# Storing every second split weight tile as one scaled float32 tile, splitting it again in the next block, and starting the later attention pairs one or two steps sooner

## The chip, the core and the metric

The kernel runs on one core of a Trainium2 chip. The core has five engines with a queue of instructions each: TensorE (PE, matmuls, with its weight loads shown apart as PEld), VectorE (DVE), ScalarE (ACT), GpSimd (POOL) and SyncE (SP). SP and POOL are used here to issue DMAs, which 16 DMA engines carry out. Work reaches an engine only when the semaphores that it waits for have been raised; an engine runs its own queue strictly in order, so an instruction that waits holds all that stand behind it. The metric is the time of one execution on the device, in microseconds, as the median of several runs.

## The reference

Attention with a learned bias of relative position, then two feed-forward layers, all in float32, for 4 batches, 8 heads, 576 positions and a head width of 64:

```python
scores = scale * np.matmul(q, k.transpose(0, 1, 3, 2))
x = (psi_rel / psi_i)[..., None]
h = np.maximum(x @ w1 + b1, 0.0)
scores = scores + (h @ w2).transpose(2, 0, 1)[None]
attn = np.exp(scores - max) ; attn = attn / (sum + 1e-09)
x = np.matmul(attn, v)                          # to [2304, 512]
gate = 1.0 / (1.0 + np.exp(-(x @ w_gate)))      # 512 -> 1536
x = (gate * (x @ w_val)) @ w_out                # 1536 -> 512
h = x @ w_in                                    # 512 -> 2048
out = (h * np.clip(h + 3.0, 0.0, 6.0) / 6.0) @ w_out2
```

## The kernel before

**Blocks.** The 576 query positions are cut into five chunks (128, 128, 128, 128, 64). For each chunk the attention of all heads and batches is computed, and the feed-forward layers then run over its tokens (512 for the first four, 256 for the last). The attention of the first chunk comes alone at the start (the lead, up to 82.8 us in the trace). After it, block k (`block`, line 953) runs the feed-forward layers of chunk k and, strewn between, the attention of chunk k + 1. Block 0 lasts from 82.80 to 329.37 us, block 1 to 563.83, block 2 to 788.97, block 3 to 993.42, block 4 to the end.

**Steps.** The feed-forward work of a block is 68 steps (`moe_steps`, line 41), each with one weight tile of 128 x 512: steps 0 to 23 are the gate and value products (G, V), 24 to 35 the first output product (Y), 36 to 45 and 54 to 59 the hidden products of the second layer (H 0 to 9 and 10 to 15), 46 to 53 and 60 to 67 its output products (O). Precision is kept by splitting every operand into a rounded part and a rest, so a product is three matmuls (line 656): rounded weight by rounded and rest of the activation, and rest of the weight by rounded activation. A step is four groups of three, twelve matmuls of 512 columns. After an H step ACT evicts the sum from PSUM (line 699), DVE forms the activation (line 700), ACT writes its rounded half gh (line 671) and DVE the rest gl (line 673). Step 61 multiplies the halves of steps 56 to 59.

**Weights.** In block 0 the weights arrive packed (wd, line 575, 512 KB a tile, a pool of 4 buffers, issued six steps ahead). `w_part` (line 592) unpacks and splits a tile in four parts: ACT scales the low bits into tpc or tpd; DVE joins them with the high bits into a plain float32 tile, in place in wd (line 607); ACT writes the rounded half of 256 times that tile into wp (lines 598 and 615); DVE writes the rest (line 618). The pair of halves in wp (a pool of 6 buffers, 512 KB) is used by the step and is also stored to memory, to wsp, by `w_store` on SP (line 634). In all later blocks `w_load` reads both halves back from wsp into wp on SP (line 581), five steps ahead; the load waits for PE's last use of the buffer. In block 0 a round of the loop issues a load for tile i + 6, the store of tile i + 2 and the split of tile i + 3.

**Attention pairs.** The attention of chunk 1, in block 0, is `chunk_att` (line 853): eight pairs of units, pair i starting at step `at[i]`. A pair's keys are split 2.1 steps before its start (`pair_split`, lines 341 and 342), its scores computed at the start, the bias added and the minimum taken by DVE (line 541), four exponentials by ACT (line 385), the division shared between ACT and DVE (lines 396 and 398), the transposes on PE (line 427) with ACT's copies out (line 431), and the product with the values (line 472) just before the next pair. The bias rows of chunk 1 are stored by POOL (line 226) and read back by SP for the first pair (line 284). In blocks 1 to 3 the transposes are done by DVE and 16 small DMAs per pair (pT, line 451), half of them or all on POOL, into one buffer that is free only after the previous pair's product.

**Order.** In block 0 the orders of PE and SP are as the program writes them; in the later blocks that of PE alone. The order of the other engines (ACT, DVE and POOL everywhere after the lead, SP in later blocks) is set when the kernel is built, by a planner that plays the program through with times of its own and lets each engine take what is ready first. Each engine then runs that order on the chip, whatever the real times are.

**Memory.** Pools are laid out one behind another. Those of the first block alone (`conv`, line 810) are closed after it, and their room is given to pools of the later blocks.

Of the kernel before, what the change touches and what calls it, by code (L numbers as in the profile page):

```python
# [9 lines left out]
F32 = mybir.dt.float32  # L10
F32R = mybir.dt.float32r
U32 = mybir.dt.uint32
# [4 lines left out]
ALU = mybir.AluOpType  # L17
# [44 lines left out]
def fused_kernel(ctx: ExitStack, tc: tile.TileContext, qd, kd, vd, tz, td, cst, iden, wpack, out):  # L62
# [28 lines left out]
        for c, (_, n) in enumerate(QC)  # L91
    ]
    wsp = dr_p.tile([NSTEP, 128, 2, 512], F32, name="wsp")

    tz_t = const.tile([128, 2 * S - 4], F32, name="tz_t")
    cst_t = const.tile([128, 3 + 32 + S // 4], F32, name="cst_t")
# [473 lines left out]
    def w_load(n):  # L570
        if n >= NC * NSTEP:
            return
        if n < NSTEP:
            wd = A["wf"].tile([128, 512, 2], U32, name="wd")
            nc.sync.dma_start(
                out=wd.rearrange("p a b -> p (a b)").bitcast(U16)[:, 0:2047], in_=wpack[n].bitcast(U16)[:, 1:2048]
            )
            wf_q[n] = wd
        else:
            wp = w_p.tile([128, 2, 4, 128], F32R, name="wp")  # L580
            nc.sync.dma_start(out=wp.rearrange("p s c m -> p s (c m)").bitcast(F32), in_=wsp[n % NSTEP])
            wq[n] = wp

    cm_q, tp_q = {}, {}
# [1 line left out]
    def w_tops(names):  # L586

        for x, name in enumerate(names):
            tp_q[x] = A["tp"].tile([128, 512], U32, name=name)
            nc.gpsimd.memset(tp_q[x], 0)  # L590

    def w_part(n, part):

        def scaled(out, x, by):
            if n < 2:
                nc.vector.tensor_scalar(out=out, in0=x, scalar1=by, scalar2=None, op0=ALU.mult)
            else:
                nc.scalar.activation(out=out, in_=x, func=AF.Copy, scale=by)  # L598

        wd = wf_q.get(n)  # L600
        if part == 0:
            top, low = (x.rearrange("p (a b) -> p a b", b=b) for x, b in (
                (wd.rearrange("p a b -> p (a b)").bitcast(BF16), 4), (tp_q[n % 2].bitcast(F16), 2)))
            scaled(low[:, :, 1], top[:, :, 2], 0.5)
        elif part == 1:
            cm_q[n] = wd[:, :, 0]
            nc.vector.scalar_tensor_tensor(
                out=cm_q[n], in0=wd[:, :, 0], scalar=13, in1=tp_q[n % 2],
                op0=ALU.logical_shift_right, op1=ALU.bitwise_or,
            )  # L610
            del wf_q[n]
        elif part == 2:
            wq[n] = w_p.tile([128, 2, 4, 128], F32R, name="wp")
            wv = wq[n].rearrange("p s c m -> p s (c m)")
            scaled(wv[:, 0], cm_q[n].bitcast(F32), 256.0)
        else:
            wv = wq[n].rearrange("p s c m -> p s (c m)")
            nc.vector.scalar_tensor_tensor(  # L618
                out=wv[:, 1], in0=cm_q.pop(n).bitcast(F32), scalar=256.0, in1=wv[:, 0].bitcast(F32),
                op0=ALU.mult, op1=ALU.subtract,  # L620
            )
            if n < 2:
                nc.sync.dma_start(out=wsp[n], in_=wv.bitcast(F32))
# [6 lines left out]
            w_part(n, part)  # L630

    def w_store(n):
        if 2 <= n < NSTEP:
            nc.sync.dma_start(out=wsp[n], in_=wq[n].rearrange("p s c m -> p s (c m)").bitcast(F32))


    ys, gs, accs, th_q, ps_q = {}, {}, {}, {}, {}
# [166 lines left out]
    def late(name, bufs):  # L804
        return pool(name, bufs, reuse_waits="tile")

    A["bo"] = late("bo", 1)
    P = dict(gu=late("gu", 12), tmp=late("tmp", 3), acc=late("acc", 4))
    A.update(k=late("k", 4), v=late("v", 4), s=late("s", 2))
    conv = ExitStack()  # L810
    for name, bufs in (("pt", 2), ("wf", 4), ("tp", 1), ("qs", 1)):
        A[name] = conv.enter_context(tc.tile_pool(name=name + "c", bufs=bufs, reuse_waits="tile"))
    ctx.enter_context(tc.issue_after(gate.ins))
    ctx.enter_context(tc.issue_after(gate_act.ins))
# [111 lines left out]
    def block_events(k):  # L926
        ev = []
        last = NSTEP - 1
        if k == 0:
            ev.append((1.0, lambda: nc.sync.dma_start(out=td_t[:, t0:], in_=td[:, t0:])))  # L930
            ev += chunk_bias(1, 1.0, 1.2, NG1 + 2)
            ev += chunk_att(1, (13, 20, 27, 33, 40, 46, 52, 58, 64))
        elif k == 1:
            d = (last - 21.0) / 9
            ev += chunk_bias4(2.0, 1.5)
# [17 lines left out]
    def block(k):  # L953
        ev = block_events(k)
        for i in range(NSTEP):
            while ev and ev[0][0] <= i:
                ev.pop(0)[1]()
            if k == 0 and i == NSTEP - 6:
                held.extend((issued[1], issued[2]))
            n = k * NSTEP + i  # L960
            if k == 0:
                if n + WA + 1 < NSTEP:
                    w_load(n + WA + 1)
                for x in range(WB - 1 if i == 0 else WB, WB + 1):
                    w_store(n + x - 1)
                    w_split(n + x)
                if i == 0:
                    for last in issued[1], issued[2]:
                        ctx.enter_context(tc.issue_after(last.ins))
            if n + WA >= NSTEP:  # L970
                w_load(n + WA)
            moe_step(k, i, P, mm_ps)
        for e in ev:
            e[1]()
# [1 line left out]
    with tc.manual_schedule(engines={ET.PE, ET.SP}):  # L976
        block(0)
    conv.close()
    A.update(ks=late("ks", 2), qs=late("qs", 2), t=late("t", 1), pt=late("pt", 1))
    with tc.manual_schedule(engines={ET.PE}), tc.issue_after(held[0].ins), tc.issue_after(held[1].ins):  # L980
        for k in range(1, NC):
            block(k)
# [64 lines left out]
```

## Time and profile before

| | |
|---|---|
| median of three runs | 1098.02 us (1096.3 to 1098.59) |
| profiled execution | 1096.07 us |
| its span | 1094.3 us |
| PE busy | 1082.1 us, 99% of the span |
| DVE, ACT, POOL busy | 645.8, 539.5, 131.7 us |
| DMA | 321.94 MB, 294 GB/s over the span |

The span runs from the first instruction of the program to its last; the execution's own time has 1.8 us around it. A matmul's end in the trace is modelled, and matmuls overlap in a pipeline, so the distance between the starts of two matmuls tells their pace, and the idle time of PE leaves a little of each late start out.

### The profile page before, as it was taken

The numbers are of one execution on the slowest core, as the hardware profiler recorded it, in microseconds if no ns is written. First come the engines' busy times: TensorE is split into PE (matmuls) and PEld (weight loads), VectorE is DVE, ScalarE is ACT, GpSimd is POOL, SyncE is SP. The second block draws the span as 40 slices with busy tenths as digits, with TensorE's granted clock in tenths as the row PEclk, the third lists the DMA queues.
The fourth block names the chain that finished last, engine by engine and source line by source line (L and its number), as shares of the span: only waits on it lengthen the run. The fifth ranks groups of instructions, "written<-read, shape, count | busy, mean of one in ns | idle before, by whom it ended". The sixth has DMA issues, their size and how long they took to land.

```text
span 1094.3 us, 19682 instructions
## 1 busy us (share of the span) xinstructions
PE 1082.1 (99%) x7042; PEld 880.4 (80%) x7042; DVE 645.8 (59%) x1530; ACT 539.5 (49%) x1066; POOL 131.7 (12%) x252
## 2 busy tenths in 40 slices
PE   9999999999999999999999999999999999999998
PEld 5777778888877787878788888788888888888897
DVE  7887777788863357886735654656252417154433
ACT  7888687798962435464523342534032214123332
POOL 2000000000010011121211111111430202031000
PEclk9999999999999999999999999999999999999999
DMA  7958999999996788999897878798995969588997
GB/s 245 354 192 314 397 357 367 381 314 386 390 333 233 234 275 283 303 305 315 286 316 254 288 253 274 244 281 244 282 295 206 304 211 286 199 254 302 369 375 269
DMA packets 118480, 321.94 MB, mean 294 GB/s; under 512 B 20720, under 2 KB 29424, under 8 KB 118384
## 3 DMA queue, kind: packets, MB, share of 16 engines
q1 hardware_dynamic: 107968, 297.09, 79.0%
q0 software_dynamic: 9152, 23.21, 7.6%
q8 instruction: 56, 0.92, 0.4%
q10 hardware_dynamic: 1264, 0.39, 0.2%
q14 instruction: 40, 0.33, 0.1%
HBM read 245.08 MB, written 51.37 MB: 271 GB/s over the span
## 4 chain that ended last, share of the span: by engine, by line
PE 83%; DMA 6%; ACT 5%; DVE 3%; issue 2%; SPq 0%; POOL 0%; DVEq 0%; ACTq 0%; POOLq 0%
PE ps L656 60%; PE ps L472 7%; PE ps L650 6%; PE ps L519 3%; DMA wsp<-wp 2%; PE ps L355 2%; PE ps L411 2%; PE ps L171 1%; DMA wd<-wpack 1%; ACT z L156 1%; ACT s L385 1%; PE ps L427 1%; DMA vt<-vd 1%; DMA biasD<-bo 1%; PE ps L525 1%
## 5 line engine op out<-in xcount | busy, mean ns | idle before, releaser
L656 PE MATMUL ps<-xyh,wp 128*128 128x512 f32 (+1 forms) x1472 | 428.9, 378 | 2.1 <-ACT wp L598 1.2
L656 PEld LDWEIGHTS ps<-xyh,wp 128*128 128x128 f32 x1472 | 263.4, 188 | 60.2 <-DVE m L541 2.7
L656 PE MATMUL ps<-gh,wp 128*128 128x512 f32 (+1 forms) x980 | 295.8, 384 | 1.1 <-ACT gh L671 1.1
L656 PE MATMUL ps<-xyl,wp 128*128 128x512 f32 x640 | 249.8, 390 | 0.4 <-DVE xyl L675 0.3
L656 PEld LDWEIGHTS ps<-gh,wp 128*128 128x128 f32 x980 | 178.8, 188 | 40.2 <-issue 2.7
L656 PE MATMUL ps<-gl,wp 128*128 128x512 f32 x448 | 175.0, 391 | 0.8 <-DVE gl L673 0.6
L451 POOL DMA_DIRECT2D pT<-t x192 | 94.4, 500 | 493.0 <-DVE t L441 153.2
L671 ACT ACTIVATE gh<-tmp 128x512 fp32r<-128x512 f32 (+1 forms) x140 | 82.1, 587 | 127.0 <-DVE tmp L694 85.0
L656 PEld LDWEIGHTS ps<-xyl,wp 128*128 128x128 f32 x640 | 120.3, 188 | 25.2 <-DVE xyl L675 1.3
L385 ACT ACTIVATE s<-s,m 128x576 f32<-128x576 f32 x144 | 110.2, 767 | 25.4 <-DVE m L541 24.0
L673 DVE TENSOR_TENSOR gl<-tmp,gh 128x512 fp32r<-128x512 f32 x112 | 76.7, 687 | 38.9 <-ACT gh L671 37.8
L656 PEld LDWEIGHTS ps<-gl,wp 128*128 128x128 f32 x448 | 84.2, 188 | 18.4 <-DVE gl L673 1.9
L472 PEld LDWEIGHTS ps<-pT,vt 128*64 128x64 f32 x1600 | 78.9, 137 | 12.9 <-issue 11.5
L472 PE MATMUL ps<-pT,vt 128*64 128x128 f32 (+1 forms) x1600 | 89.1, 265 | 0.1
L700 DVE SCALAR_TENSOR_TENSOR tmp<-tmp,ps 128x512 f32<-128x512 f32 (+1 forms) x80 | 50.1, 629 | 54.8 <-ACT tmp L699 53.2
L694 DVE SCALAR_TENSOR_TENSOR tmp<-tmp,ps 128x512 f32<-128x512 f32 x48 | 32.7, 682 | 74.7 <-PE ps L656 73.7
L699 ACT ACTIVATE tmp<-ps 128x512 f32<-128x512 f32 (+1 forms) x80 | 43.9, 549 | 43.9 <-PE ps L656 43.5
L398 DVE TENSOR_SCALAR s<-s,r 128x576 f32<-128x576 f32 x128 | 61.4, 516 | 1.9
L497 ACT ACTIVATE xyh<-ps 128x256 fp32r<-128x256 f32 (+1 forms) x44 | 15.2, 344 | 94.4 <-PE ps L472 94.4
L724 POOL DMA_DIRECT2D outT<-acc x40 | 27.7, 737 | 267.6 <-DVE acc L715 247.7
L618 DVE SCALAR_TENSOR_TENSOR wp<-wd,wp 128x512 fp32r<-128x512 f32 x68 | 46.7, 688 | 21.4 <-ACT wp L598 20.8
L541 DVE CUSTOM_DVE_ANT_0 s<-ps,bm,m 128x320 f32<-128x320 f32 x112 | 56.1, 545 | 0.0
(112 smaller groups left out, 1169.6 us busy)
## 6 DMA issues: line engine op xcount, KB each, us to landing
wp<-wsp SPq DMA_DIRECT2D x272, 512.0 KB, 5.3
wsp<-wp SPq DMA_DIRECT2D x68, 512.0 KB, 7.4
wd<-wpack SPq DMA_DIRECT2D x68, 511.8 KB, 7.0
vt<-vd SPq DMA_DIRECT2D x80, 320.0 KB, 5.5
kt<-kd SPq DMA_DIRECT2D x80, 288.0 KB, 5.8
pT<-t POOLq DMA_DIRECT2D x192, 72.0 KB, 4.9
pT<-t SPq DMA_DIRECT2D x128, 72.0 KB, 4.4
bm<-biasD SPq DMA_DIRECT2D x15, 576.0 KB, 6.2
```

Of the source, the lines that this page charges most:

```text
L385: nc.scalar.activation(out=s[:, h], in_=s[:, h], func=AF.Exp, scale=-1.0, bias=d["m"][:, h:h + 1], accum_out=r[:, h:h + 1],)
L398: nc.vector.tensor_scalar(out=s[:, h], in0=s[:, h], scalar1=r[:, h:h + 1], scalar2=None, op0=ALU.mult)
L451: (nc.sync if p[0][0] < 4 and i > 1 else nc.gpsimd).dma_start(out=pt[32 * q:32 * q + 32, i].rearrange("j u t i -> j (u t i)"), in_=t[32 * ...
L472: nc.tensor.matmul(out=po[64 * h:64 * h + 64, n * a:n * a + n], lhsT=vt[:, v], rhs=pt[:, m * a:m * a + m, k, :], start=(t == 0), stop=(t = ...
L541: nc.vector.tensor_tensor_reduce(out=d["s"][:, h, j0:j1], in0=x, in1=bm_q[c, hp][:, h, j0:j1], scale=-(D ** -0.5), scalar=top, op0=ALU.add ...
L618: nc.vector.scalar_tensor_tensor(out=wv[:, 1], in0=cm_q.pop(n).bitcast(F32), scalar=256.0, in1=wv[:, 0].bitcast(F32), op0=ALU.mult, op1=AL ...
L650: nc.tensor.matmul(out=o, lhsT=w[:, c, :], rhs=x, start=(first and c == 0 and w is wh), stop=(last and c == 3 and w is wh),)
L656: nc.tensor.matmul(out=ps[:, 0:nt], lhsT=w[:, c, :], rhs=x[:, 0:nt], start=(first and c == 0 and i == 0), stop=(last and c == 3 and i == 2),)
L671: nc.scalar.activation(out=hi, in_=src, func=AF.Copy, scale=scale)
L673: nc.vector.tensor_tensor(out=lo, in0=src, in1=hi.bitcast(F32), op=ALU.subtract)
L699: nc.scalar.activation(out=t, in_=ps, func=AF.Relu, bias=3.0)
L700: nc.vector.scalar_tensor_tensor(out=t, in0=t, scalar=6.0, in1=ps, op0=ALU.min, op1=ALU.mult)
```

## The change

For the 20 even tiles from 2 to 40 (`in_whole`), block 0 forms the plain float32 tile in a buffer of its own (cm, two buffers) and not in place in wd, and `w_store` stores that tile, 256 KB, to a new place in memory, wsf, where before both halves went to wsp. The split in block 0 stays. In block 1 the load of such a tile reads 256 KB from wsf into one half of wp. `w_again` splits it there, two steps ahead of its use: one ACT pass and one DVE pass of 128 x 512. `w_keep` then stores both halves to wsp, one step ahead of the use, on POOL's queue; blocks 2 to 4 read wsp as before.

In block 0 the starting steps of the attention pairs move: pairs 0 and 1 stay at 13 and 20, pairs 2 to 7 go from 27, 33, 40, 46, 52, 58 to 26, 32, 38, 44, 50, 56, and the end of the last from 64 to 63. The pool of keys has two buffers in block 0 instead of four, and is made anew, with four, for the later blocks.

```diff
@@ w_load
         else:
             wp = w_p.tile([128, 2, 4, 128], F32R, name="wp")
-            nc.sync.dma_start(out=wp.rearrange("p s c m -> p s (c m)").bitcast(F32), in_=wsp[n % NSTEP])
+            wv = wp.rearrange("p s c m -> p s (c m)").bitcast(F32)
+            if in_whole(n - NSTEP):
+                nc.sync.dma_start(out=wv[:, 1], in_=wsf[n - NSTEP])
+            else:
+                nc.sync.dma_start(out=wv, in_=wsp[n % NSTEP])
             wq[n] = wp
+    def in_whole(n):
+        return 2 <= n < 42 and n % 2 == 0
@@ w_part
         elif part == 1:
-            cm_q[n] = wd[:, :, 0]
+            cm_q[n] = A["cm"].tile([128, 512], U32, name="cm") if in_whole(n) else wd[:, :, 0]
@@ w_store
-        if 2 <= n < NSTEP:
+        if in_whole(n):
+            nc.sync.dma_start(out=wsf[n], in_=cm_q.pop(n).bitcast(F32))
+        elif 2 <= n < NSTEP:
             nc.sync.dma_start(out=wsp[n], in_=wq[n].rearrange("p s c m -> p s (c m)").bitcast(F32))
+    def w_again(n):
+        if in_whole(n - NSTEP):
+            wv = wq[n].rearrange("p s c m -> p s (c m)")
+            f = wv[:, 1].bitcast(F32)
+            nc.scalar.activation(out=wv[:, 0], in_=f, func=AF.Copy, scale=256.0)
+            nc.vector.scalar_tensor_tensor(
+                out=wv[:, 1], in0=f, scalar=256.0, in1=wv[:, 0].bitcast(F32), op0=ALU.mult, op1=ALU.subtract
+            )
+    def w_keep(n):
+        if in_whole(n - NSTEP):
+            nc.gpsimd.dma_start(out=wsp[n - NSTEP], in_=wq[n].rearrange("p s c m -> p s (c m)").bitcast(F32))
@@ pools
-    A.update(k=late("k", 4), v=late("v", 4), s=late("s", 2))
+    A.update(v=late("v", 4), s=late("s", 2))
-    for name, bufs in (("pt", 2), ("wf", 4), ("tp", 1), ("qs", 1)):
+    for name, bufs in (("pt", 2), ("wf", 4), ("tp", 1), ("qs", 1), ("k", 2), ("cm", 2)):
...
-    A.update(ks=late("ks", 2), qs=late("qs", 2), t=late("t", 1), pt=late("pt", 1))
+    A.update(k=late("k", 4), ks=late("ks", 2), qs=late("qs", 2), t=late("t", 1), pt=late("pt", 1))
@@ block_events
-            ev += chunk_att(1, (13, 20, 27, 33, 40, 46, 52, 58, 64))
+            ev += chunk_att(1, (13, 20, 26, 32, 38, 44, 50, 56, 63))
@@ block
             if n + WA >= NSTEP:
                 w_load(n + WA)
+                w_keep(n + 1)
+                w_again(n + 2)
             moe_step(k, i, P, mm_ps)
```

## Rows read from the trace of the kernel before

**Rows 1.** Page, part 1: busy time, share of the span, instructions.

```profile
PE 1082.1 (99%) x7042; PEld 880.4 (80%) x7042; DVE 645.8 (59%) x1530; ACT 539.5 (49%) x1066; POOL 131.7 (12%) x252
```

**Rows 2.** Busy time by stretch: length, PE, PEld, DVE, ACT, POOL; clock, DMA, GB/s.

```profile
82.80:329.37 246.57, 243.04 (x1516) 198.48 (x1515) 191.07 (x423) 198.47 (x359) 6.30 (x10) 1.00 0.98 360
...
329.37:455.00 125.63, 125.63 (x728) 99.63 (x727) 67.58 (x161) 51.64 (x98) 13.25 (x26) 1.00 0.79 260
...
455.00:563.83 108.83, 108.12 (x732) 86.09 (x730) 76.09 (x180) 50.29 (x100) 23.76 (x46) 1.00 0.96 309
...
563.83:788.97 225.14, 224.80 (x1393) 184.22 (x1392) 123.36 (x300) 82.48 (x160) 39.12 (x75) 1.00 0.85 267
```

**Rows 3.** Timeline of PE alone, steps of the first block: start, us, instruction, count.

```profile
107.40 0.61 PE L656 MATMUL ps<-xyh,wp 128*128 128x512 f32 x2
...
114.20 0.62 PE L656 MATMUL ps<-xyh,wp 128*128 128x512 f32 x2
```

**Rows 4.** Same view: idle before matmuls, steps 17 and 18 (brackets: us, releaser).

```profile
136.83 0.50 PE L656 MATMUL ps<-xyh,wp 128*128 128x512 f32 x1 [1.19 <-ACT wp L598]
...
137.99 0.73 PE L656 MATMUL ps<-xyh,wp 128*128 128x512 f32 x2 [0.43 <-DVE wp L618]
...
142.52 0.73 PE L656 MATMUL ps<-xyh,wp 128*128 128x512 f32 x2 [0.52 <-DVE wp L618]
```

**Rows 5.** Same view: idle before matmuls, step 61.

```profile
305.24 0.50 PE L656 MATMUL ps<-gh,wp 128*128 128x512 f32 x1 [0.48 <-ACT gh L671]
...
305.97 0.50 PE L656 MATMUL ps<-gl,wp 128*128 128x512 f32 x1 [0.22 <-DVE gl L673]
...
306.95 0.50 PE L656 MATMUL ps<-gh,wp 128*128 128x512 f32 x1 [0.25 <-ACT gh L671]
...
307.81 0.51 PE L656 MATMUL ps<-gl,wp 128*128 128x512 f32 x1 [0.37 <-DVE gl L673]
```

**Rows 6.** Waits of PE over the span: total us, times, longest.

```profile
PE ps L656 <- ACT wp L598: 1.2, 1, 1.2
...
PE ps L656 <- DVE wp L618: 0.9, 2, 0.5
```

**Rows 7.** Chain that ended last, 112 to 140 us: start, us, what.

```profile
112.94 8.49 DMA biasD<-bo
```

**Rows 8.** Waits of the SP queue, 83 to 330 us: total us, times, longest.

```profile
SPq L575 <- DVE wp L618: 90.5, 44, 5.5
...
SPq L284 <- DMA biasD<-bo: 6.8, 1, 6.8
```

**Rows 9.** DMA issues: engine, op, count, KB each, median us to landing.

```profile
wp<-wsp SPq DMA_DIRECT2D x272, 512.0 KB, 5.3
...
wsp<-wp SPq DMA_DIRECT2D x68, 512.0 KB, 7.4
...
kt<-kd SPq DMA_DIRECT2D x80, 288.0 KB, 5.8
...
biasD<-bo POOLq DMA_DIRECT2D x8, 303.5 KB, 7.8
```

**Rows 10.** Timeline of ACT alone, 286 to 309 us.

```profile
297.43 0.76 ACT L385 ACTIVATE s<-s,m 128x576 f32<-128x576 f32 x1
...
301.09 0.57 ACT L699 ACTIVATE tmp<-ps 128x512 f32<-128x512 f32 x1
...
304.58 0.61 ACT L671 ACTIVATE gh<-tmp 128x512 fp32r<-128x512 f32 x1
```

**Rows 11.** Groups by form: busy us, mean ns of one, idle before it.

```profile
L598 ACT ACTIVATE wp<-wd 128x512 fp32r<-128x512 f32 x66 | 44.0, 667 | 14.0 <-DVE wd L607 12.5 <-PE ps L656 1.1
...
L618 DVE SCALAR_TENSOR_TENSOR wp<-wd,wp 128x512 fp32r<-128x512 f32 x68 | 46.7, 688 | 21.4 <-ACT wp L598 20.8
```

**Rows 12.** Timeline of POOL alone, 400 to 435 us.

```profile
404.30 3.95 POOL L451 DMA_DIRECT2D pT<-t  x8 [72.25 <-DVE tmp L694]
...
429.42 4.15 POOL L451 DMA_DIRECT2D pT<-t  x8 [21.17 <-PE ps L472]
```

More of the change, by code (lines that the diff above doesn't have):

```diff
@@ L93, in fused_kernel @@
     wsp = dr_p.tile([NSTEP, 128, 2, 512], F32, name="wsp")
+    wsf = dr_p.tile([NSTEP, 128, 512], F32, name="wsf")
     tz_t = const.tile([128, 2 * S - 4], F32, name="tz_t")
@@ L618, in w_part @@
             nc.vector.scalar_tensor_tensor(
-                out=wv[:, 1], in0=cm_q.pop(n).bitcast(F32), scalar=256.0, in1=wv[:, 0].bitcast(F32),
+                out=wv[:, 1], in0=cm_q[n].bitcast(F32), scalar=256.0, in1=wv[:, 0].bitcast(F32),
                 op0=ALU.mult, op1=ALU.subtract,
```

## The prediction

> **What bounds the kernel now.** I read first the page's busy times: PE, TensorE's matmul engine, is busy 1082.1 us of a span of 1094.3, no other engine over 645.8 [rows 1]. A busy PE could still be a slow one, so I next read the timeline of PE: in a quiet stretch a group of three matmuls starts every 0.68 us (eleven groups, ten intervals, from 107.40 to 114.20), so a weight step of twelve takes 2.72 us [rows 3]. Inside the blocks that spacing hardly changes, at a granted clock of 1.00 [rows 2]. The matmuls are the same before and after, so this change can only remove or add slips, places where PE starts late. Where they lie is read from the busy times by stretch: the first block, 246.57 us long, has 3.53 us without a matmul; the second block 0.00 and 0.71 in its two parts; the third 0.34 [rows 2]. In the first block they are in two places: 1.19 + 0.43 + 0.52 us at steps 17 and 18 [rows 4], and 0.48 + 0.22 + 0.25 + 0.37 us at step 61 [rows 5]. The recorded end of a matmul is 0.16 us after the point at which the next could start (0.39 long, 0.23 apart; 0.27 behind a first one of 0.50), so the slips are a little more than the idle: 2.14 + 3 x 0.16 = 2.6 us, and 1.32 + 0.16 + 0.27 + 0.16 + 0.27 = 2.2 us. Together 4.8 us, 0.44% of the span. That is all the first block can give; the later blocks hold about 1 us idle.
>
> What ends each slip differs. At steps 17 and 18 PE waits for the split weight tile wp, and all waits of PE for it in the span are these three [rows 4, 6]. Behind it: the SP queue stood 6.8 us, because the bias rows it wanted to read back had not landed; their store took 8.49 us [rows 7, 8]. No weight load goes out meanwhile. The DMA engines are 0.98 busy in this block at 360 GB/s [rows 2], so a landing is mostly queueing. At step 61 PE waits for gh and gl, an activation of step 58, not a weight [rows 5]: ACT ran the four exponentials of the last pair from 297.43 to 301.1, only then evicted that step's sum (301.09), and wrote its gh at 304.58 [rows 10].
>
> **The change, part by part.**
>
> Stores in block 0. Twenty tiles (2, 4, .. 40) are stored with 256 KB instead of 512: 20 x 0.262 MB = 5.2 MB less, of 246.57 us x 360 GB/s = 89 MB, or 6%. Before the first slip the stores of tiles 8, 10, 12 and 14 are among what is in flight: 4 x 0.262 MB at 360 GB/s is 2.9 us less queue [rows 2]. How much sooner the bias store and the loads behind it land no row shows. From above: all 2.9 us, and then the whole 2.6 us slip goes. From below: nothing, since the bias store is on the POOL queue and the halved ones on SP's; it could also be a loss, if the 2 KB rows are moved worse, which I bound by 0.5 us. Of the 512 KB store the median landing is 7.4 us, of the 288 KB load 5.8 [rows 9], so halving a transfer takes about 1.6 us off its own landing, nearer to the upper end. I take 2.0 us of the 2.6.
>
> The Trainium skill speaks against this. Its page "DMA: Bandwidth & Descriptors", section "Anatomy of one DMA — SWDGE (gpsimd) path", fits a DMA's time as about 2.0 us fixed plus bytes at 436 GB/s, so that 256 KB less would save an estimated 0.6 us, and the first slip would lose 0.6 instead of 2.0 us. The rows here, 7.4 against 5.8, do not follow it [rows 9], as the engines are 0.98 busy.
>
> The early release. A whole tile is formed in a buffer of its own (cm, 2 buffers), so the packed load's buffer is free after the first of DVE's two passes over it (line 607), not the second (line 618). The SP queue waits for that second pass 44 times, 90.5 us in all [rows 8]. The gain is inside the 2.0 above. The price: cm's buffer returns only when its store lands, four steps or 10.9 us later at the least; against a landing of 7.4 us [rows 9] the cover is 3.5 us. If it is gone, DVE waits at the head of its queue, and the eviction of sums behind it, 1 to 2 us each time.
>
> Pairs sooner. Pairs 2 to 7 start 1, 1, 2, 2, 2 and 2 steps sooner and the last product one step sooner, 2.72 to 5.4 us each; no work is added. Pair 7's four exponentials then lie 5.4 us ahead of 297.43, and ACT can evict steps 58 and 59 as they end: of the 2.2 us I take 1.9 (bounds 0 and 2.2). The price is tighter pairs from step 20 on. ACT is busy 198.47 and DVE 191.07 of 246.57 us [rows 2], so the work fits, but weight tiles may be late around steps 26 to 31. Below: nothing; above: the one step by which pair 2 moves, 2.7 us. I take 0.6. The k pool has 2 buffers instead of 4: the next pair's loads, issued when a pair starts, need that pair's split, which stands 2.1 steps (5.7 us) earlier; I cost it at nothing, at up to 1 us if ACT splits late.
>
> Block 1. Twenty ACT passes of 0.667 and twenty DVE passes of 0.688 us [rows 11] are 13.3 and 13.8 us. They fall in steps 0 to 39, about 329 to 455, where ACT has 51.64 and DVE 67.58 busy of 125.63 us and PE has no idle at all [rows 2]. So 0 on the path while the loads come five steps (13.6 us) ahead: 5.3 to land [rows 9] and 1.4 for the two passes leave 6.9 us. DMA: 10.5 MB more written by POOL and 5.2 MB less read, 5.2 MB in 125.63 us, 42 GB/s on top of 260 at a share of 0.79 [rows 2]; it fits. A store on POOL has a nearest row of 7.8 us (303.5 KB, in the loaded block) [rows 9]. Issued once the split is ready, some 6.9 us ahead of its step, it lands 0.9 us into that step, and PE holds the buffer 2.72 us anyway; so SP, behind whose wait for the buffer the next weight and attention loads are queued, loses nothing. Queued behind the store on POOL are the transposing copies pT, which the attention product waits for; an issue of about 0.5 us (3.95 us for eight [rows 12]) hides there.
>
> A new order on ACT, DVE, SP and POOL in the later blocks, which a planner sets: between the 1 us that is idle there (a gain) and 3 us; I take 0.5 us loss, as little is left to win.
>
> Sum: -2.0 - 1.9 + 0.6 + 0.5 = -2.8 us. The profiled execution took 1096.07 us (span 1094.3 and 1.8 around it), so it would be 1093.3. The median of the runs, 1098.02, lies 1.95 above that execution, so on the median it is **1095.2 us**. About 0.2%, 2.2 us, is what a measurement of this kernel can tell from no change.
>
> **Rivals.**
>
> The relief is too small (no change). If landings have mostly a fixed part, the first slip keeps 2.0 of its 2.6 us; the end's 1.9 is gained, and 0.6 + 0.5 lost, with another 1 us late at steps 26 to 31: 0.6 + 1.9 - 2.1 = 0.4 us gain, 1097.6. For it: SP's 6.8 us stand on a store of the other queue, which the change leaves whole. Against: everything behind it is queued with halved stores.
>
> Both slips and the later idle vanish: 4.8 + 1 = 5.8 us, 1092.2. It needs no new slip at all.
>
> Tighter pairs cost more than they give (slower). Pair 2's earlier start puts ACT behind, and weights at steps 26 to 31 come late by 2.7 us, twice, while only 1.9 us is gained at the end: +3.5, 1101.5. It decides once ACT's lead on a weight tile, when pair 2 starts, is under one step.
>
> POOL's queue (slower). Its pT copies stand waiting for the previous pair's product: 21.17 us without an issue ahead of 429.42 [rows 12]. A weight store ordered behind such a wait holds its buffer, SP stops on it, and PE runs out after the five steps loaded ahead: 21.2 - 13.6 = 7.6 us, 1105.6. It decides when the planner puts one store behind a pT whose product is more than five steps off. Against: a store is ready long before such a pT, so an order by readiness has it first.
>
> **How the numbers follow.** Forecast 0.45; both vanish 0.07; relief too small 0.28; tighter pairs 0.12; POOL 0.08. Faster: 0.45 + 0.07 = 0.52; same 0.28; slower 0.12 + 0.08 = 0.20. The range runs from 1091.5, everything gained and a run like the profiled one, to 1101.5, the tighter pairs' price; outside lie POOL's 0.08 and some 0.08 of the tails. The forecast alone has 1093 to 1096.5.
>
> **What would show it.** Right: in the busy times by stretch the first block is about 3 us shorter than 246.57, with under 1.5 us without a matmul; no PE wait for wp near step 17; the wait of SP for the bias rows under 6.8 us; at the end of the block the exponentials ahead of step 58; stretch 329 to 455 still without idle on PE. Wrong: waits of PE for wp at steps 26 to 31 (tighter pairs), PE waits for a wp load or for ACT's second split in block 1 with POOL idle before a store (POOL's queue), DVE waiting for the store of cm (the early release), or an unchanged slip at step 17 (relief too small).

## The result: 1112.5 us, slower, and the profile after

The changed kernel takes 1112.5 us in the median (1110.84 to 1115.31) against 1098.03: a ratio of 1.0135, 95% interval 1.0113 to 1.0158. The forecast was 1095.2, with 1101.5 as the upper end of its range. The profiled execution of after took 1111.45 us, its span 1109.7.

The page's first part, and the busy times of the blocks (length, then busy time and instructions of PE, PEld, DVE, ACT, POOL; clock, DMA share, GB/s), to be held against [rows 1, 2]. The first line is block 0, the next two block 1 cut 125.63 us after its start, as in [rows 2] (not at the same step), the last block 2.

```profile
PE 1085.3 (98%) x7042; PEld 881.7 (79%) x7042; DVE 657.5 (59%) x1550; ACT 547.5 (49%) x1086; POOL 143.9 (13%) x272
...
83.94:335.35 251.41, 244.25 (x1515) 199.57 (x1515) 190.15 (x423) 195.86 (x359) 6.33 (x10) 0.99 0.92 330
335.35:460.98 125.63, 118.72 (x641) 93.71 (x641) 72.35 (x157) 54.82 (x103) 20.25 (x38) 0.97 0.85 288
460.98:578.96 117.98, 117.24 (x820) 93.33 (x817) 83.75 (x203) 57.50 (x114) 28.25 (x54) 1.00 0.93 304
578.96:804.40 225.44, 224.88 (x1394) 184.13 (x1393) 123.35 (x300) 82.55 (x160) 39.25 (x75) 1.00 0.85 268
```

Read by steps (start of the same weight step, after less before, from each block's start), PE is level to step 16, 2.9 us ahead at step 19, where the first slip stood, and 4.8 us behind at the end of block 0 (251.41 against 246.57). Block 1 is level to step 31, where 8.3 us are lost at one place, and ends 9.15 us longer (243.61 against 234.46). Blocks 2 to 4 differ by under 0.3 us. The lead was 1.1 us longer in this execution, with a wait of PE of 1.2 us for a load of keys. Of the twelve profiled executions with a smaller pool of keys, two or three buffers (this one among them), six have a lead of 83.9 to 85.3 us, the others of 82.8 to 83.1; the five with four buffers have 82.8 to 83.2. So about a microsecond may belong to the lead; no run shows whether the pool is its cause.

The waits of PE over the span (total us, times, longest) say where:

```profile
PE ps L520 <- DVE xyl L499: 6.7, 1, 6.7
PE ps L428 <- ACT pT L432: 4.7, 3, 2.8
...
PE ps L428 <- ACT s L397: 1.3, 2, 0.6
```

No wait for wp is left [rows 6]. The new waits are all for attention work: in block 0 for the copies out of the transposes (line 432, before 431), in block 1 for the rest of a pair's queries (line 499).

**The place in block 1.** Timelines of after around it give start, us, instruction, and in brackets the idle time before and its releaser. SP's queue first:

```profile
428.23 0.45 SPq L285 DMA_DIRECT2D bm<-biasD  x1
428.90 0.34 SPq L306 DMA_DIRECT2D kt<-kd  x1
429.50 0.61 SPq L298 DMA_DIRECT2D qt<-qd  x1
430.22 0.56 SPq L584 DMA_DIRECT2D wp<-wsf  x1
```

POOL's queue in the same stretch:

```profile
425.95 0.54 POOL L660 DMA_DIRECT2D wsp<-wp  x1 [7.00 <-DVE wp L653]
430.37 0.72 POOL L660 DMA_DIRECT2D wsp<-wp  x1 [3.87 <-DVE r L393]
```

ACT:

```profile
439.41 0.63 ACT L652 ACTIVATE wp<-wp 128x512 fp32r<-128x512 f32 x1 [8.78 <-DMA wp<-wsf]
441.19 0.63 ACT L652 ACTIVATE wp<-wp 128x512 fp32r<-128x512 f32 x1 [1.15 <-DMA wp<-wsf]
441.73 0.37 ACT L498 ACTIVATE xyh<-ps 128x256 fp32r<-128x256 f32 x1
```

DVE:

```profile
440.07 0.69 DVE L653 SCALAR_TENSOR_TENSOR wp<-wp 128x512 fp32r<-128x512 f32 x1 [4.69 <-ACT wp L652]
441.85 0.69 DVE L653 SCALAR_TENSOR_TENSOR wp<-wp 128x512 fp32r<-128x512 f32 x1 [1.09 <-ACT wp L652]
442.46 0.42 DVE L499 TENSOR_TENSOR xyl<-ps,xyh 128x256 fp32r<-128x256 f32 x1
```

PE, which wants the pair's scores:

```profile
442.93 0.58 PE L520 MATMUL ps<-kh,qh 64*128 64x256 f32 x1 [6.68 <-DVE xyl L499]
```

SP issues the 256 KB load of a plain tile at 430.22, behind the bias rows, keys and queries of the next pair; it lands 9.1 us later, at 439.3. Its tile, 34, is not needed by PE before step 34, and PE is at step 31. But ACT's queue holds its second split next: ACT stands 8.78 us at its head. Behind it and the split of tile 36 on ACT is the copy xyh (line 498, 0.37 us), behind its partner on DVE the rest xyl, and PE's scores wait for that. Ready work of under a microsecond stood behind a load that was early for its own user.

The load itself left late, and for the same reason. An earlier second split had stood 5.34 us on ACT ahead of the copies of the keys (line 324), and SP's next load of keys waited 4.5 us for the rest of those keys (ACT's timeline, and SP's waits from 418 to 437 us):

```profile
424.28 0.63 ACT L652 ACTIVATE wp<-wp 128x512 fp32r<-128x512 f32 x1 [5.34 <-DMA wp<-wsf]
424.82 1.24 ACT L324 ACTIVATE kh<-kt 128x576 fp32r<-128x576 f32 x2
...
SPq L306 <- DVE kl L325: 4.5, 1, 4.5
```

The load of tile 34, behind that one on SP, so left 94.9 us after the block's start, against 89.7 in before, where the 512 KB landed in 7.2 us. Over this stretch (335 to 461 us) ACT's waits have one line that no row of before answers to:

```profile
ACT wp L652 <- DMA wp<-wsf: 56.2, 17, 10.2
```

**The places in block 0.** The longest of them, in PE's timeline of after:

```profile
237.67 1.79 PE L428 MATMUL ps<-id_t,s 128*128 128x128 f32 x9 [2.81 <-ACT pT L432]
```

ACT's timeline ahead of it:

```profile
224.73 0.79 ACT L607 ACTIVATE tpd<-wd 128x512 f16<-128x512 bf16 x1 [5.86 <-DMA wd<-wpack]
...
236.84 0.78 ACT L432 ACTIVATE pT<-ps 128x768 f32<-128x768 f32 x1
238.05 0.46 ACT L432 ACTIVATE pT<-ps 128x384 f32<-128x384 f32 x1
```

The same pattern: ACT stands 5.86 us at the unpacking of tile 45, which waits for its packed load, then has a backlog, and the copy out of the transposes comes late.

**The halved transfers.** DMA issues over the span (count, KB, median us to landing), against [rows 9]:

```profile
wsp<-wp SPq DMA_DIRECT2D x48, 512.0 KB, 7.3
wsp<-wp POOLq DMA_DIRECT2D x20, 512.0 KB, 4.2
wsf<-cm SPq DMA_DIRECT2D x20, 256.0 KB, 7.7
wp<-wsf SPq DMA_DIRECT2D x20, 256.0 KB, 4.9
```

A store of 256 KB lands no sooner than one of 512. And of the waits of SP's queue in block 0, the one for the bias rows has grown, against 6.8 us in [rows 8]:

```profile
SPq L285 <- DMA biasD<-bo: 9.6, 1, 9.6
```

### The profile page after: what moved, and what is told of

The parts are those of the page before. It is cut to its first block, busy times and chain, and to the rows that moved or that the text cites. A ratio compares the mean times of both kernels' runs of the same rounds, so it can differ in the third digit from the quotient of the medians.

```text
span 1109.7 us, 19738 instructions
## 1 busy us (share of the span) xinstructions
PE 1085.3 (98%) x7042; PEld 881.7 (79%) x7042; DVE 657.5 (59%) x1550; ACT 547.5 (49%) x1086; POOL 143.9 (13%) x272
## 4 chain that ended last, share of the span: by engine, by line
PE 68%; DMA 4%; DVE 2%; ACT 2%; issue 0%; SPq 0%; DVEq 0%; ACTq 0%
PE ps L682 53%; PE ps L676 6%; PE ps L473 4%; PE ps L520 3%; DMA wp<-wsf 2%; DMA wd<-wpack 1%; PE ps L172 1%; PE ps L526 1%; DMA wsp<-wp 1%; DMA wp<-wsp 1%; DVE s L542 0%; ACT s L386 0%; PE ps L180 0%; ACT wp L607 0%; DVE kl L325 0%
## 5 line engine op out<-in xcount | busy, mean ns | idle before, releaser
L442 DVE STREAM_TRANSPOSE t<-s 128x1152 f32<-128x1152 f32 x40 | 54.2, 1368 | 0.3
```

Source lines behind the costliest of these rows:

```text
L442: nc.vector.transpose(out=tn_q[0][:, :, x], in_=st[u]["s"].rearrange("p h j -> p (h j)").rearrange("p (t q j) -> p q t j", q=4, j=32),)
```

## Experiments

Each is the kernel before or after with one thing changed. Ratios are to the kernel before as run beside it, with the 95% interval; block lengths are from the profiled execution of each (before: 246.57 and 234.46 us).

### Which part costs

**e1: all but the sooner pairs.**

```diff
-ev += chunk_att(1, (13, 20, 26, 32, 38, 44, 50, 56, 63))
+ev += chunk_att(1, (13, 20, 27, 33, 40, 46, 52, 58, 64))
```

> The changed kernel with the pairs of block 0 back at their old starting steps (13, 20, 27, 33, 40, 46, 52, 58, 64); stores, early release and second split as changed. Theory A (the loss in block 0, some 7.8 us from step 36 on, is the sooner pairs; the loss in block 1, some 9 us at steps 31 and 32, is the second split standing at the head of ACT's queue before its load has landed): block 0 comes back to about 244 us, under the 246.57 of before because the slip at step 17 stays away; block 1 keeps its loss of 8 to 9 us; in all 1103 to 1106. Rival B (the loss in block 0 is the early release: SP runs ahead and then stands in front of the value loads): block 0 stays at 250 to 252 us, in all 1110 to 1113.

1114.52 us, 1.0145 (1.0126 to 1.0165); block 0 252.30, block 1 242.49. The tighter pairs are not the loss: without them it is no smaller (16.3 us over the kernel before, against 14.5; the intervals overlap).

**e2: the kernel before with the sooner pairs alone** (the diff of e1, reversed).

> The kernel before with the new starting steps of the pairs alone. Theory A: block 0 loses 5 to 8 us from step 36 on and keeps the slip at step 17, block 1 is as before (234.5 us): 1101 to 1106. Rival B: the sooner pairs cost nothing without the early release and the slip at step 61 shrinks: 1096 to 1098.

1093.54 us, 0.9961 (0.9946 to 0.9976); block 0 243.19, block 1 234.51. PE's idle at step 61 [rows 5] is gone. This is the fastest kernel of the study, faster than both.

**e3: the early release, whole stores, old pairs, nothing in block 1.**

```diff
     def w_store(n):
-        if in_whole(n):
-            nc.sync.dma_start(out=wsf[n], in_=cm_q.pop(n).bitcast(F32))
-        elif 2 <= n < NSTEP:
+        if 2 <= n < NSTEP:
...
-                w_keep(n + 1)
-                w_again(n + 2)
```

> The kernel before with the buffer cm for the 20 even tiles (so the packed load's buffer is free after DVE's first pass) and the k pool of 2, and nothing else: both halves stored in block 0 as before, no second split, old pairs. Theory A: the early release alone removes the slip at step 17, 2 to 3 us of block 0, nothing is lost: 1094.5 to 1097. If the halved stores removed it: block 0 about 246.6 us as before, 1097 to 1099. Rival B: a loss in block 0 of 4 to 8 us with SP standing for the value loads.

1100.70 us, 1.0026 (1.0016 to 1.0036); block 0 249.61. PE is 1.06 us ahead of before at step 19 and then loses 4.1 us, 3.6 of them at steps 58 to 62, where the granted clock is 0.50 for 3.4 us.

**e9: the kernel before with two key buffers in block 0.**

```diff
-    A.update(k=late("k", 4), v=late("v", 4), s=late("s", 2))
+    A.update(v=late("v", 4), s=late("s", 2))
-    for name, bufs in (("pt", 2), ("wf", 4), ("tp", 1), ("qs", 1)):
+    for name, bufs in (("pt", 2), ("wf", 4), ("tp", 1), ("qs", 1), ("k", 2)):
...
```

> The kernel before with one thing changed: the pool of keys has two buffers in block 0 instead of four (old pair steps, whole stores, joins in place). In e3 that and the early release together made block 0 3.0 us longer. If the smaller pool is what costs (a pair's keys are loaded later, ACT splits them late): block 0 about 249 to 250 us and 1100 to 1101 us in all. If the early release is what costs: block 0 at 246.6 and 1098 us. If each has a part: between.

1099.08 us, 1.0015 (1.0001 to 1.0030); block 0 249.88. The interval leaves the smaller key pool 0.1 to 3.3 us. Block 0 can't be held against e3's 249.61: the profiled execution took 1102.44 us, 3.4 more than the median, and in two stretches of its block 0, of 3.4 us each from 140.8 and 311.4, the granted clock is 0.50, which costs up to 3.4 us. PE's idle time in it is 3.91 us, against 3.53 in before. What the early release adds (1.0026 against 1.0015) is not resolved.

**e12: e3 with the sooner pairs** (the two diffs above).

> e3 with the new pair steps: the early release for 20 tiles, two key buffers, whole stores, nothing in block 1, and the sooner pairs. e3 lay 2.5 us over the kernel before, e2 (pairs alone) 4.5 us under it. If the two add: 1096.2 us, block 0 about 246. If e3's loss is the crowded end of block 0 that the sooner pairs clear: 1093 us, block 0 243 or less. If sooner pairs need the keys earlier than two buffers allow: over 1098.

1096.88 us, 0.9998 (0.9987 to 1.0009); block 0 247.0. The two roughly add: 1.0026 x 0.9961 is 0.9987, the lower end of the interval.

**e7: e3 with halved stores.** Block 1 on loads the neighbouring tile's halves for the 20 tiles, so its numbers are computed with wrong weights.

```diff
     def w_store(n):
+        if in_whole(n):
+            nc.sync.dma_start(out=wsf[n], in_=cm_q.pop(n).bitcast(F32))
-        if 2 <= n < NSTEP:
+        elif 2 <= n < NSTEP:
```

> The kernel before with the block 0 part of the change alone: buffer cm, k pool of 2, halved stores, old pairs; no second split and no stores in block 1, where the neighbouring odd tile is loaded in place of each of the 20 (wrong weights). Against the run with cm and k pool alone (249.6 us in block 0) it tells what the halved stores do. Theory A: the planner, which sees less traffic, places the unpacking of tiles 40 to 51 and 58 to 66 some two to four steps earlier in ACT's order, and block 0 takes 251 to 253 us as with the whole change and old pairs; block 1 is 234.5; in all 1101 to 1105. Rival E (fewer bytes help, the loss in block 0 has to do with the later part): block 0 at 244 to 249.6, 1095 to 1100.

1105.6 us, 1.0076 (1.0053 to 1.0099); block 0 252.67, block 1 234.47. PE is 2.93 us ahead at step 19, as in after, then 6.1 behind at the end.

**e10: the kernel before with halved stores alone.**

```diff
     def w_store(n):
+        if in_whole(n):
+            nc.sync.dma_start(out=wsp[n, :, 0], in_=wq[n].rearrange("p s c m -> p s (c m)")[:, 0].bitcast(F32))
-        if 2 <= n < NSTEP:
+        elif 2 <= n < NSTEP:
```

> The kernel before with one thing changed: of the even tiles 2 to 40 only the rounded half is stored (256 KB), from the same buffer and at the same place of the SP queue; nothing of the pairs, the pools or block 1. Block 1 then loads the neighbouring tile's two halves in place of such a tile's, so the numbers from block 1 on are computed with wrong weights at the same cost; that part is left out of the change on purpose. It is the prediction's first term alone. The prediction: the first slip loses 2.0 of 2.6 us, 1096 us. Rival, a smaller store lands no sooner: the slip stays, 1098. Second rival, suggested by e7 against e3 (3.1 us longer): smaller stores make the queue worse, block 0 about 249.5 and 1101 us.

1102.71 us, 1.0047 (1.0032 to 1.0063); block 0 252.91. The first term of the prediction's sum, alone, costs 5.4 us. The waits of PE in block 0 (total us, times, longest):

```profile
PE ps L427 <- ACT pT L431: 2.8, 1, 2.8
PE ps L662 <- ACT gh L677: 1.4, 1, 1.4
PE ps L662 <- DVE gl L679: 1.2, 1, 1.2
```

Its stores on SP among the DMA issues (count, KB, median us to landing):

```profile
wsp<-wp SPq DMA_DIRECT2D x48, 512.0 KB, 7.4
wsp<-wp SPq DMA_DIRECT2D x20, 256.0 KB, 6.4
```

The first slip is gone and larger ones have come after it. Here halving takes 1.0 us off a landing, where the prediction had 1.6. The estimate of 0.6 us that the prediction worked out from the Trainium skill (page "DMA: Bandwidth & Descriptors", section "Anatomy of one DMA — SWDGE (gpsimd) path", a fit for DMAs that GpSimd issues, while these are issued by SP) is 0.4 us off on the other side; the row lies between the two.

### Why smaller stores cost: the order on ACT

Up to block 1 only 20 stores differ between e10 and before: they are half as large and need the rounded half alone, not DVE's rest. Yet ACT's instructions run in another order. Counted from the traces: how many evictions of H sums ACT does before it unpacks a tile.

```text
tile                  40  42  45  47  49  58  60  62  64
before                 2   4   5   8  10  11  13  14  16
after                  0   0   2   4   6  10  10  11  12
e10, smaller stores    0   1   3   4   6  10  10  12  14
e12, whole stores      1   2   6   8   8  11  12  12  15
e13, order put back    1   3   6   8  10  11  13  15  16
```

With smaller stores the unpacking comes one to four evictions sooner. ACT's waits for packed loads in block 0 grow with it, from 5.6 us in before to 9.7 in e10. Whether the order or the smaller stores cost was tried by pinning the order:

**e8: the whole change, pinned loosely**: from round 38 on a tile's unpacking and splitting stands behind the last eviction of a G or H sum but one (`evs` lists those evictions).

```diff
-                    w_split(n + x)
+                    if i >= 38:
+                        with tc.issue_after(evs[-2].ins):
+                            w_split(n + x)
+                    else:
+                        w_split(n + x)
```

> The changed kernel with one thing fixed in the planner's order: from step 38 of block 0 on, the unpacking and splitting of the tile three steps ahead may be issued on ACT only behind ACT's eviction of the second last step with one, about where the kernel before has it. Theory A: the slips of the transposes and at the end of block 0 go, block 0 takes 241 to 245 us instead of 251.4; block 1 keeps its loss; in all 1102 to 1106. Rival B (the early release and SP's waits): block 0 stays at 249 to 252, 1109 to 1113.

1112.03 us, 1.0116 (1.0080 to 1.0153). Block 0 falls from 251.41 to 249.02, with two stretches of 3.4 us at half the clock in place of one; block 1 rises to 249.44, since the later order changes with it (5.1 and 4.8 us of PE idle). The total tells little, block 0 does.

**e13: e10 pinned** (as e8, with `i >= 37` and `evs[-1]`).

> e10 (the kernel before with only the rounded half stored of the even tiles 2 to 40; block 1 on is computed with neighbouring tiles' weights, left out of the change on purpose) with the order of ACT put back: from round 37 on, the unpacking and splitting of a tile stands behind the eviction of the step before, so that tile 49 is unpacked behind 10 evictions of H steps as in the kernel before (6 in e10) and tile 60 behind 13 (10 in e10). If ACT's order is the cause of e10's loss: the slip at 242 us (2.76) goes, the first slip stays gone, block 0 at 244 to 246.5 us and 1095 to 1097.5 us. If the smaller stores themselves cost (transfers that are moved worse): block 0 stays at 252 to 253 us and 1102 us. e8, which held the order less tightly in the whole change, came to 249.0.

1099.03 us, 1.0015 (0.9999 to 1.0030); block 0 248.10 instead of 252.91. The order is most of e10's loss: 4.8 of 6.3 us in block 0, 3.7 of 5.4 in the medians. Block 0 of e10, then of e13 (columns as at the top):

```profile
82.82:335.73 252.91, 247.14 (x1516) 201.87 (x1516) 190.13 (x423) 196.91 (x359) 6.30 (x10) 0.98 0.92 332
...
82.79:330.89 248.10, 244.11 (x1515) 200.04 (x1515) 190.93 (x423) 197.37 (x359) 6.30 (x10) 0.99 0.92 336
```

Of the 4.8 us, 1.8 are idle time of PE (5.77 less 3.99); most of the rest is the clock, granted at 0.50 for 10.2 us of e10's block and for 3.4 of e13's. ACT's waits for packed loads are as long as in e10 (9.6 us), so it is not those that the pin took away; by what path the order cost is shown only at the places above. I had also expected the slip at 242 us to go; it stayed. PE's transposes of that pair in the timeline of before:

```profile
237.73 1.14 PE L427 MATMUL ps<-id_t,s 128*128 128x128 f32 x9
241.58 1.20 PE L427 MATMUL ps<-id_t,s 128*128 128x128 f32 x9
```

The same in e13, with the line of ACT's copies between them:

```profile
234.86 1.14 PE L427 MATMUL ps<-id_t,s 128*128 128x128 f32 x9
...
241.88 2.12 PE L427 MATMUL ps<-id_t,s 128*128 128x128 f32 x9 [2.33 <-ACT pT L431]
...
241.02 1.18 ACT L431 ACTIVATE pT<-ps 128x768 f32<-128x768 f32 x2
```

In e13 PE is 2.9 us earlier at the first nine (the first slip gained), but ACT's copies come at 241.02, against 240.72 in before: ACT is no earlier. Why, its timeline in e13 shows:

```profile
224.60 0.69 ACT L341 ACTIVATE z<-kt 128x576 fp32r<-128x576 f32 x1 [2.03 <-DMA kt<-kd]
...
228.96 0.78 ACT L385 ACTIVATE s<-s,m 128x576 f32<-128x576 f32 x1 [2.83 <-DVE m L541]
```

It stands 2.03 us for a load of keys, then 2.83 us for the minimum from DVE, and works without a gap from there to the copies. Before has the split of keys later there (236.35), with no wait. ACT was not fuller in this stretch: from 214 to 243 us it is busy 25.39 us in before (the first line, busy times with ACT the fifth figure) and 23.47 in e13 (the second):

```profile
214.00:243.00 29.00, 29.00 (x187) 24.19 (x186) 24.38 (x54) 25.39 (x48) 0.00 (x0) 1.00 0.96 340
...
214.00:243.00 29.00, 26.42 (x169) 21.47 (x169) 23.89 (x52) 23.47 (x44) 0.00 (x0) 0.98 0.70 229
```

The gain of the first slip is handed back where PE meets ACT. The pin put back the unpacking, not the whole order; whether the place of the key split alone holds ACT here, no run tried.

**e14: e13 with tiles 14 and 16 put back too** (the condition becomes `10 <= i <= 16 or i >= 37`).

> e13 with the order put back at tiles 14 and 16 as well (behind 6 and 7 evictions of G steps as in the kernel before, 5 and 6 in e10; 12, 15, 17 and 19 stay as in e10). If the first slip went because less was queued (the prediction's reason): it stays gone, the same time as e13. If it went because tiles 14 and 16 are unpacked one eviction earlier: part of the 2.1 us idle at steps 17 and 18 comes back, and 1 to 2 us more than e13.

1098.32 us, 1.0007 (0.9995 to 1.0019); block 0 247.30. The first slip comes back in part (PE's timeline):

```profile
140.28 0.51 PE L663 MATMUL ps<-xyh,wp 128*128 128x512 f32 x1 [0.57 <-ACT wp L602]
...
141.26 0.73 PE L663 MATMUL ps<-xyh,wp 128*128 128x512 f32 x2 [0.25 <-DVE wp L622]
```

At step 19 PE is 1.59 us ahead of before; in e13 it was 2.53, in e10 2.81. So 0.9 us of the first slip, against e13, came from two tiles being unpacked one eviction earlier, not from a shorter queue. In the medians it costs nothing that can be told. Block 0 is 0.8 us shorter than e13's only because e13's has 3.4 us at half the clock (up to 1.7 us lost) and this one none; its idle time is 0.6 us longer.

### Why the second split costs: its wait

**e5: the second split reads ready data.** The two passes stand in the program where they stood, on a constant instead of the loaded tile, with the rest written to a scratch tile, so block 1's weights for those tiles are not formed.

```diff
-            f = wv[:, 1].bitcast(F32)
+            f = tz_t[:, 0:512]
```

> The changed kernel (new pairs) with the second split's wait for its load taken away: ACT and DVE make the same two passes of 128x512 into the same time of block 1, but read an old constant tile, and DVE's goes to a free part of it; the loads from wsf and the stores on POOL stay (the weights of these 20 tiles are then not the right ones). Theory A (the load at the head of ACT's and DVE's queues costs block 1 its 9 us): block 1 comes back to 234.5 to 236 us from 243.6, block 0 stays at about 251.4: 1102 to 1105. Rival C (the added work or the added traffic): block 1 stays at 241 to 244, 1110 to 1113.

1104.06 us, 1.0053 (1.0031 to 1.0075); block 0 252.05, block 1 234.46, which is before's to 0.01 us, with the loads, stores and all forty passes still there. The work and its transfers cost block 1 nothing; the wait, in the order that comes with it, costs 9.15 us. For the order changed too: the planner, for which the constant is always ready, moved some passes, and of the two directly ahead of the pair's copy one was left. So e5 does not part the wait from the order; e6 below does, at that place.

**e4: the second split and its store one step later in the program.**

```diff
-                w_keep(n + 1)
-                w_again(n + 2)
+                w_keep(n)
+                w_again(n + 1)
```

> The changed kernel with the second split and its store each placed one step later in the program (split one step ahead of its use instead of two). Theory A: the loads have 2.7 us more to land before the split stands in ACT's and DVE's queues, so the waits of ACT for them, 56.2 us in 17 places, shrink to under 35 us and the loss in block 1 falls from 9 us to 0 to 4; block 0 is unchanged: 1103 to 1109. Rival C (the second split's mere work and the stores on POOL cost block 1 its 9 us): block 1 stays at about 243.6 us, 1111 to 1113.

1113.31 us, 1.0141 (1.0123 to 1.0158); block 1 245.16, idle 1.56 us at 403 and 5.27 at 443. ACT, DVE, SP and POOL run the same instructions in block 1 in the same order as in after. The place in the program does not set their order; the planner does, and so this run is after once more and tells nothing of a later split.

**e6: no stores of the split tiles by POOL** (blocks 2 to 4 use the neighbouring tile's weights).

```diff
-                w_keep(n + 1)
```

> The changed kernel without the stores on POOL in block 1 (the later blocks load the neighbouring odd tile in place of each of the 20, so they work on wrong weights). Theory A: ACT still waits for the loads, block 1 stays at 239 to 244 us, 1107 to 1113. Rival D (POOL's 10.5 MB of stores make the loads late): block 1 comes back to 234.5 to 236, 1102 to 1105.

1106.47 us, 1.0078 (1.0053 to 1.0103); block 0 253.55, block 1 236.87. ACT still waits for the loads nearly as long in all (its waits, 335 to 461 us):

```profile
ACT wp L652 <- DMA wp<-wsf: 50.1, 17, 10.3
```

but 6.7 of the 9.15 us are gone. The same two splits stand ahead of the pair's copy, with shorter waits (ACT's timeline in e6):

```profile
432.82 0.63 ACT L652 ACTIVATE wp<-wp 128x512 fp32r<-128x512 f32 x1 [3.72 <-DMA wp<-wsf]
435.60 0.63 ACT L652 ACTIVATE wp<-wp 128x512 fp32r<-128x512 f32 x1 [2.15 <-DMA wp<-wsf]
```

Tile 34's load left 90.6 us after the block's start, not 94.9, and landed in 5.7 us, not 9.1. The copy came in time, and PE loses 0.2 us at this place instead of 8.3 (another 2.2 by step 40). So at the same place of ACT's queue the length of the wait decides, and most waits there are harmless. The earlier split that held the copies of the keys in after stands behind them here; whether that or the missing stores made the load come sooner is not parted.

**e11: the change for tiles 2 to 14 only, three key buffers.**

```diff
-        return 2 <= n < 42 and n % 2 == 0
+        return 2 <= n < 16 and n % 2 == 0
...
-("k", 2), ("cm", 2)):
+("k", 3), ("cm", 2)):
```

> The kernel after with the halved stores, the early release and the second split for tiles 2 to 14 only (7 instead of 20) and three key buffers in block 0 instead of two. In block 1 their second splits lie in steps 0 to 14, before the attention work of that block, so if the loss of block 1 is a split that waits at the head of ACT's queue with attention work behind it, block 1 is back at 234.5 us. If any second split costs, block 1 keeps a third of its 9 us, 237.5. Block 0: the first slip gone (2.95) and the sooner pairs' 3.4 gained, if those add: 241 to 243 and 1091 to 1093 us, under both kernels and under e2. If the smaller pool and the early release cost whatever the number of tiles: 1096 to 1098.

1094.96 us, 0.9984 (0.9974 to 0.9994); block 0 244.18, block 1 234.49. In steps 0 to 14 of block 1 no copy of a pair is queued close behind the splits (work for the bias rows is), and block 1 loses nothing. In block 0 the first slip is gone, but the block is 1.0 us longer than e2's.

**e15: e11 with the order pinned as in e13.**

> e11 (halved stores, early release and second split for tiles 2 to 14 only, three key buffers, sooner pairs) with the order of ACT put back from round 37 on, as in e13. If that order is what still held e11 back in block 0 (slips of 0.37, 0.99 and 0.40 us at 236, 256 and 309 us): block 0 at 241 to 242.5 us instead of 244.2, and 1092 to 1093.5 us, at or under e2's 1093.5. If those slips belong to the sooner pairs or the keys: as e11, 1095 us. If holding the splits back starves the later steps: over 1097.

1096.08 us, 0.9985 (0.9973 to 0.9998); block 0 244.83. No better: what holds e11 behind e2 is not that order. Whether it is the keys or the ACT time itself stays open.

## Why the prediction was wrong, point by point

**The step that failed most: the second split "0 on the path".** Its cover of 6.9 us was reckoned for the tile against its own use, and the tile was never late: PE waits for no wp in after. What was left out is who stands behind the split. The prediction asked that of POOL's queue and of DVE's wait for cm, not of the two engines that the new wait was put on. Its work is free, as claimed (e5). The wait costs 9.15 us in block 1, and 8.0 in the medians (after 14.5 over the kernel before, e5 6.5), the change of order in e5 included. The term 5.3 us for a landing was also a median: in the burst it was 9.1, after a load that left 5 us late because another second split had held ACT.

**The halved stores, -2.0.** The first slip went, all 2.9 us of it, so the term looks right at its place. Alone the edit is +5.4 us (e10), through an order that the prediction considered only for the later blocks (+0.5): smaller stores change the planner's times, and ACT's order in block 0 with them. The reason given holds only in part: SP's wait for the bias rows is shorter in e10 (5.9 us against 6.8 [rows 8]) but longer in after (9.6), a 256 KB store landed 1.0 us sooner (e10) or not at all (after), and 0.9 us came from the order (e14). The slip went as forecast; what it gained did not last to the end of the block.

**Pairs sooner, -1.9 and +0.6.** Right in sign and place, too small in size: alone 4.7 us faster in the medians, 3.4 in block 0, where the two terms give 1.3. The price at steps 26 to 31 did not come. In the whole change only 1.8 of it is left (e1 against after, within the noise of both).

**The keys, 0 to 1.** 1.8 us in the medians (interval 0.1 to 3.3; e9). Where they are lost is not shown: of the 6.4 us that e9's profiled execution is longer than before's, 1.7 are in the lead, where PE waits 1.7 us for a load of keys, and 3.3 in block 0, which the two falls of the clock are enough to explain. The price put on the early release did not come: DVE has no wait for a store of cm. That it is free is not resolved.

**The sum.** In the medians, each against the kernel before beside it: pairs -4.7 (e2), keys and early release +2.4 (e3), halved stores +5.4 (e10), second split +8.0 (e5): +11.1. The sooner pairs lose 2.9 of their 4.7 in the whole change (e1); that makes 14.0, and 14.5 was measured. These are single parts from different comparisons, with intervals of 1 to 2.5 us to either side, so the last two microseconds are not resolved.

**The rivals.** The relief was not too small at its place: no wait for wp is left. POOL's queue had the right kind of event, a queue held up at its head, on the wrong engine: POOL waits for DVE's splits, and no pT stood ahead of a late store at the place of the loss. Tighter pairs are refuted by e1 and e2. Of the signs of being wrong none came as written: PE waited neither for a wp load nor for the second split, but for a copy queued behind it. Of the signs of being right, stretch 329 to 455 without idle on PE failed (6.91 us), as did the shorter block 0.

## What to carry to other kernels

When a wait is added, ask of the engine it is put on what is next in its queue, and who waits for that; the slack of the waiting data itself says nothing. Where an order is planned at build time from modelled times, the size of a transfer is an input to that order: look at the order of the instructions before and after, and compare it tile by tile, before costing anything by durations. Time gained on one engine was handed back here at its next meeting with another that was no earlier (e13); look for that point before counting the gain. And hold block lengths of single executions against their medians and their granted clock: e9's block 0 was 3.3 us longer with hardly more idle time.

## What the runs showed of the hardware

After idle times of PE the granted clock in several places fell to 0.50 (1.2 of 2.4 GHz) for 3.4 or 6.8 us (10.2 once, in e4), and PE paid again when the wait had ended. Busy times around the slip in block 1 of after (columns as at the top, the clock third from the end):

```profile
430.00:436.20 6.20, 6.20 (x62) 4.46 (x60) 5.35 (x12) 0.63 (x3) 0.72 (x1) 1.00 0.97 291
436.20:442.90 6.70, 0.05 (x1) 0.00 (x0) 1.74 (x4) 2.34 (x5) 0.54 (x1) 0.77 1.04 374
442.90:446.60 3.70, 3.67 (x24) 3.34 (x25) 3.60 (x14) 2.14 (x5) 3.07 (x7) 0.50 0.99 355
446.60:450.00 3.40, 3.40 (x16) 2.73 (x16) 3.33 (x12) 3.40 (x10) 1.41 (x3) 0.99 0.96 269
```

The 6.7 us of idle became 8.3 us of delay: 3.7 us at half the clock are up to 1.85 us lost. Before has no such fall but in its last 4 us; e13 has one after an idle of 2.33 us, e14 none after one of 2.30, so the same slip can cost 1.7 us more or not. So block lengths of single executions can differ by that much at the same idle time. And a store of 512 KB issued by POOL landed in 4.2 us in block 1, where one issued by SP took 7.3 in block 0; the DMA engines' share there was 0.85 and 0.92, and no run tells that from the queue.
